# Pooled attention, then a SiLU layer: denominators and numerators of the attention grouped otherwise within a tile

## The chip, the cores and the metric

One Trainium2 chip, one core. The metric is the device time of one execution in microseconds. Engines: PE (TensorE) does the matrix products, ACT (ScalarE) the exponentials, logarithms, SiLU and some copies, DVE (VectorE) sums and products of tiles, POOL (GpSimd) some sums and most loads, SP the stores. Products land in PSUM, which has eight banks; everything else lies in SBUF.

## The reference

Keys and values are averaged over eight neighbouring rows, a softmax attention of 576 queries over 72 pooled keys follows, for 8 batches of 8 heads of width 64. The result, 4608 tokens of 512, goes through two matrix products with a SiLU between them (512 to 2048 to 512).

```python
k_p = k.reshape(B, H, Sp, pool, D).mean(axis=3)
v_p = v.reshape(B, H, Sp, pool, D).mean(axis=3)
scores = scale * np.matmul(q, k_p.transpose(0, 1, 3, 2))
scores = scores - np.max(scores, axis=-1, keepdims=True)
attn = np.exp(scores)
attn = attn / (np.sum(attn, axis=-1, keepdims=True) + 1e-09)
out = np.matmul(attn, v_p)
# x: tokens x 512, heads side by side
h = x @ w_in
g = h * (1.0 / (1.0 + np.exp(-h)))
return g @ w_out
```

## The kernel before

The tokens are worked in nine tiles of 512 (t = 0 to 8), each in two halves. `up` multiplies the tile by `w_in` and applies SiLU; `down`, or from tile 1 on `down_quarters`, multiplies by `w_out` and stores. Three quarters of the hidden units in `up` (from tile 1 on) and all of `down_quarters` use seven products in place of eight, with sums of the operands made on DVE: `x_sum` (L444) for the token side, `h_sum` (L605) for the hidden side. The seven products collect in three PSUM banks named P, Q and R, tag "mm". Product 2 goes to P and 5 to Q, r_sb (ACT) and rr_sb (DVE) take them out, 1 goes to R and t_sb (DVE) takes it out, then 4 and 7 go to P and 3 and 6 to Q. The four results go to `o_sb` by L666, L671, L675 and L679, in this order, and SP stores them.

The attention of batch t + 1 is worked in `down_quarters` of tile t, in small matmuls between the large ones. Its 576 queries are cut into three thirds (`visits`) of 192 tokens, two groups of heads side by side, 384 columns. For each third: `scores` (16 matmuls into four banks, then four exponentials on ACT into `es`), `denominators` (four matmuls with a matrix of ones into one bank, then on ACT `lnd`, a logarithm, and `rec`, the exponential of its negative), and `numerators` (16 matmuls into two banks, then two products with `rec` on DVE, which write `xT`, the tokens of later tiles). These use the PSUM tag "at", which has five banks, used in turn; `up` uses the same five for the P and Q of its units. Tile t + 1 covers the last tokens of batch t and the first of batch t + 1, so in tiles 1 to 5 the last third of a batch is not needed in the next tile, and parts of it are left to that tile's `down_quarters`.

The order on every engine is the order in which the program issues its instructions. `spread` sets it: the 112 matmuls of `down_quarters` are steps 0 to 111, each filler has a step, and a filler is issued as soon as the next step comes up; fillers with the same step keep the order in which they were listed. A filler's ACT, DVE and DMA instructions get their place in their engines' queues at the same moment. Each engine waits in its own order for what its next instruction needs.

In tiles 2 to 5, `down_quarters` has four groups of attention matmuls: scores of third 0 (step 1); denominators of the last third of the batch before, denominators of third 0 and scores of third 1 (33); denominators of third 1, numerators of third 0 and of the last third of the batch before (56); numerators of third 1, into one "mm" and one "at" bank, and scores of third 2 (79.5 and 80). Tile 1 has the same without the batch before. Tile 6 has its scores at 1, 33 and 75, denominators and numerators of its last two thirds at 97 and 101, and also works off batch 6's last third at 33 and 56. Tiles 7 and 8 have no attention. The sums `x_sum` for the next tile's `up` stand at step 92, in tile 6 at 98, in tile 7 at 44.

At the start of the attention ACT loads its table for exponential and logarithm (L400), at the end of it the one for SiLU (L403). In the next `up` POOL first waits for the last `x_sum` (L196, "gate"), then pools k (L190, L193), issues a load of the next k, pools v, and issues the other loads.

Of the kernel before, what the change touches and what calls it, by code (L numbers as in the profile page):

```python
# [36 lines left out]
def kernel(  # L37
# [53 lines left out]
    def ps_tile(shape, dtype, tag, name):  # L91
        return psum.tile(shape, dtype, tag=tag, bufs=banks[tag], name=name)
# [259 lines left out]
    def denominators(b, segs, on_dve=False):  # L352
        st = batches[b]
        w = width(segs)
        es = st["es", segs]
        den_ps = ps_tile([128, 512], FP32, "at", "den_ps")
        for s in range(4):
            nc.tensor.matmul(  # L358
                den_ps[32 * s : 32 * (s + 1), :w],
                lhsT=ones, rhs=es[:, s, :], start=True, stop=True,  # L360
            )
        rec = mid.tile([128, VW], FP32, tag="rec", bufs=4, name="rec")[:, :w]
        if on_dve:
            nc.vector.reciprocal(rec, den_ps[:, :w])
        else:
            lnd = mid.tile([128, VW], FP32, tag="lnd", name="lnd")[:, :w]
            nc.scalar.activation(lnd, den_ps[:, :w], func=AF.Ln)  # L367
            nc.scalar.activation(rec, lnd, func=AF.Exp, scale=-1.0)
        st["rec", segs] = rec
# [262 lines left out]
    def down_quarters(t, fillers, last=False):  # L632
        step = spread(fillers, 7 * 2 * KQ)
        ps = {
            n: ps_tile([128, 2, CQ], FP32, "mm", f"o_ps{n}") for n in "RPQ"
        }
        bank = {2: "P", 5: "Q", 1: "R", 4: "P", 3: "Q", 7: "P", 6: "Q"}
        begun = set()

        def product(n, k0, k1, cs=(0, 1)):  # L640
            b = bank[n]
            for kt in range(k0, k1):
                for c in cs:
                    next(step)
                    nc.tensor.matmul(  # L645
                        ps[b][:, c, :], lhsT=left(n, kt, c), rhs=W_OUT[n][:, kt, :],
                        start=b not in begun,
                        stop=kt == k1 - 1, skip_group_check=True,
                    )
                    begun.add(b)  # L650

        add, sub = ALU.add, ALU.subtract
        tt = nc.vector.tensor_tensor
        KA = KQ // 2
        product(2, KA, KQ)
        product(5, KA, KQ)
        product(2, 0, KA)
        nc.scalar.copy(r_sb, ps["P"])
        product(5, 0, KA)
        tt(out=rr_sb, in0=ps["Q"], in1=r_sb, op=add)  # L660
        for cc in ((0,), (1,)) if last else ((0, 1),):
            cs = slice(cc[0], cc[-1] + 1)
            product(1, 0, KQ, cc)
            tt(out=t_sb[:, cs], in0=ps["R"][:, cs], in1=rr_sb[:, cs], op=sub)
            product(4, 0, KQ, cc)
            nc.scalar.copy(o_sb[1][:, cs, LO], ps["P"][:, cs])  # L666
            tail = last and cc == (1,)
            if tail:
                store(t, 3, LO, (nc.gpsimd,))
            product(3, 0, KQ, cc)  # L670
            nc.vector.tensor_copy(out=o_sb[0][:, cs, HI], in_=ps["Q"][:, cs])  # L671
            if tail:
                store(t, 1, HI)
            product(7, 0, KQ, cc)
            tt(out=o_sb[0][:, cs, LO], in0=ps["P"][:, cs], in1=t_sb[:, cs], op=add)  # L675
            for c in cc:
                store(t, c, LO if tail else FULL, (nc.scalar if tail else nc.sync,))
            product(6, 0, KQ, cc)
            tt(out=o_sb[1][:, cs, HI], in0=ps["Q"][:, cs], in1=t_sb[:, cs], op=add)  # L679
            for c in cc:  # L680
                if tail:
                    store(t, 3, HI, both)
                else:
                    store(t, 2 + c, FULL, (nc.gpsimd if last else nc.sync,))
        for _ in step:
            pass
# [105 lines left out]
    for t in range(NT):  # L792
# [43 lines left out]
        if a < B:  # L836
            q_at = [4, 14, 4, 8] if t > 1 else [24, 25, 26, 2] if t else [82, 84, 86, 88]
            if t == 0:
                for j in range(2):
                    f_up.append((44 + 8 * j, lambda j=j: slot_sums("k", j)))  # L840
                    f_up.append((72 + 8 * j, lambda j=j: select_k(1, j)))
                    f_up.append((72 + 8 * j, lambda j=j: copy_k(1, j)))
                    f_down.append((20 + 10 * j, lambda j=j: slot_sums("v", j)))
                    f_down.append((37 + 3 * j, lambda j=j: select_v(1, j, "at")))
                    f_down.append((37 + 3 * j, lambda j=j: copy_v(1, j)))
            elif t == 1:
                for j in range(2):
                    f_up.append((0, lambda j=j: slot_sums("k", j, halves=True)))
                    f_up.append((22, lambda j=j: select_k(2, j)))
                    f_up.append((23, lambda j=j: copy_k(2, j)))  # L850
                    f_down.append((8, lambda j=j: slot_sums("v", j, halves=True)))
                    f_down.append((40, lambda j=j: select_v(2, j, "at")))
                    f_down.append((41, lambda j=j: copy_v(2, j)))
            else:
                f_up.append((1, behind_x_sums))
                f_up.append((1, lambda: pool_k(a)))
                if a + 1 < B:
                    f_up.append((2, lambda: load_one(a + 1, "k")))
                f_up.append((2, lambda: pool_v(a)))
                f_up.append((40, lambda: k_transpose(a)))  # L860
            for n in range(4):
                f_to = f_down if t and n >= (2 if t > 1 else 3) else f_up
                f_to.append((q_at[n], lambda n=n: q_transpose(a, n % 2, n // 2)))
            if t == 0:
                f_down.append((0, lambda: load_half_2("k", 0)))
                f_down.append((0, lambda: load_q(2)))
                f_down.append((0, lambda: load_half_2("k", 1)))
                for half in range(2):
                    f_down.append((31, lambda half=half: load_half_2("v", half)))
                for y in range(2):  # L870
                    for n in U_W:
                        f_down.append((6, lambda y=y, n=n: unit_weight_sum(y, n)))
            elif a + 1 < B:
                if t == 1:
                    f_up.append((0, lambda: load_one(a + 1, "k")))
                f_to, at = (f_up, 4) if t > 1 else (f_down, 11)
                f_up.append((5 if a + 1 == B - 1 else 0, lambda: load_q(a + 1)))
                f_to.append((at, lambda: load_one(a + 1, "v")))
                f_up.append((5, lambda: load_rest(a + 1, "k")))
                f_to.append((at + 2, lambda: load_rest(a + 1, "v")))  # L880
            f_down.append((0, attn_tables))

            if t:
                sc_at, den_at, nu_at = (1, 33, 80), (33, 56, 97), (56, 79.5, 101)
                if t == B - 2:
                    sc_at, nu_at = (1, 33, 75), (56, 97, 101)
            else:
                sc_at, den_at, nu_at = (1, 16, 30), (16, 30, 44), (44, 55, 56)
            later = 0 < t < B - 2
            if 1 < t < B - 1:  # L890
                f_down.append((den_at[0], lambda: denominators(a - 1, visits[2])))
            for n, sg in enumerate(visits):
                if n < 2 or not later:
                    f_down.append((den_at[n], lambda sg=sg: denominators(a, sg)))
                f_down.append((sc_at[n], lambda sg=sg: scores(a, sg)))

            for n, sg in enumerate(visits):
                tags = ("mm", "at") if later and n == 1 else ("at", "at")
                if n < 2 or not later:
                    f_down.append(  # L900
                        (nu_at[n], lambda sg=sg, tags=tags: numerators(a, sg, tags))
                    )
                if n == 0 and 1 < t < B - 1:
                    f_down.append((nu_at[n], lambda: numerators(a - 1, visits[2])))
        if 0 < t < B:
            for n in (4, 1, 3, 7, 6):
                f_down.append((44 if t == B - 1 else 98 if t == B - 2 else 92, lambda n=n: unit_x_sum(t + 1, n)))
        if t == 1:
            def unit_weight_tiles():
                k_w = big.tile([128, 4, 2, 256], BF16, tag="k_raw2", name="w_sum12")  # L910
# [43 lines left out]
```

## Time and profile before

| | us |
|---|---|
| median of 3 runs | 282.37 |
| lowest, highest | 282.14, 282.44 |
| the profiled execution's own time | 282.37 |
| its span | 280.6 |
| tile 2, 81.31 to 110.40 | 29.09 |
| tile 3, 110.40 to 139.49 | 29.09 |
| tile 4, 139.49 to 168.62 | 29.13 |
| tile 5, 168.62 to 197.70 | 29.08 |
| tile 6, 197.70 to 227.60 | 29.90 |
| tile 7, 227.60 to 252.49 | 24.89 |

| engine | busy, us | share of the span |
|---|---|---|
| PE | 273.7 | 98% |
| DVE | 221.1 | 79% |
| ACT | 189.2 | 67% |
| POOL | 98.3 | 35% |

A tile is taken here from the first matmul of its `up` to that of the next. In the lines below, a row of a timeline gives the start in us, the length, the engine, the line of the kernel, the operation with its result and sources, their shapes, and how many equal instructions were merged; in brackets stands how long the engine was idle before it and which instruction ended that. The ends of matmuls are modelled, and they overlap, so that distances of starts say more than lengths. A row of the waits gives who waited for whom, the total in us, how many times, and the longest.

### The profile page before, as it was taken

What the parts mean: (1) busy time and instruction counts of PE and PEld (TensorE: products, weight loads), DVE (VectorE), ACT (ScalarE), POOL (GpSimd) and SP (SyncE); (2) the same over time, 40 slices, a digit from 0 to 9 for tenths busy, and PEclk for the clock granted to TensorE, in tenths of its full rate; (3) what the DMA queues carried; (4) which work ended last, traced back from release to release, by engine and by line L of the source; (5) the groups of instructions that cost most, each with busy time, mean ns of one, the idle gap of its engine ahead of it and who ended that gap; (6) DMA issues with size and microseconds to landing.
All of it is one profiled execution on the core that took longest, in us unless ns stands there. A gap on an engine that the chain in (4) does not pass through costs nothing.

```text
span 280.6 us, 7165 instructions
## 1 busy us (share of the span) xinstructions
PE 273.7 (98%) x2877; PEld 203.7 (73%) x2877; DVE 221.1 (79%) x415; ACT 189.2 (67%) x369; POOL 98.3 (35%) x104
## 2 busy tenths in 40 slices
PE   8999998999999999999999999999999999999995
PEld 4448444577888777867888788677877878788784
DVE  4996858997898967796879696978788588966982
ACT  1788767468567974797579866995699668426810
POOL 8655217232168233931293109940910000000001
PEclk9999999999999999999999999999999999999999
DMA  7999999897459797789467805998320032005004
GB/s 215 277 258 241 208 313 204 220 197 117 115 75 236 186 130 148 184 167 129 78 161 187 126 11 132 204 112 129 87 66 2 2 94 58 0 5 138 11 2 151
DMA packets 31313, 37.71 MB, mean 134 GB/s; under 512 B 10352, under 2 KB 22256, under 8 KB 31280
## 3 DMA queue, kind: packets, MB, share of 16 engines
q0 software_dynamic: 23920, 27.03, 52.6%
q1 hardware_dynamic: 6928, 9.58, 12.1%
q10 hardware_dynamic: 432, 0.66, 0.6%
q8 instruction: 22, 0.36, 0.6%
q14 instruction: 11, 0.09, 0.1%
HBM read 36.70 MB, written 9.44 MB: 164 GB/s over the span
## 4 chain that ended last, share of the span: by engine, by line
PE 78%; DMA 12%; DVE 4%; POOL 2%; ACT 1%; issue 1%; POOLq 0%; DVEq 0%
PE o_psP L645 16%; PE o_psQ L645 15%; PE u_psP L477 11%; PE hp_ps L537 10%; PE u_psQ L477 10%; DMA raw<-in_v_dram 9%; PE o_psR L645 5%; DMA raw<-in_k_dram 3%; PE u_psR L477 3%; PE sc_ps L340 3%; PE nu_ps L384 2%; PE den_ps L358 1%; DVE w_sum L623 1%; DVE xT L393 1%; ACT lnd L367 1%
## 5 line engine op out<-in xcount | busy, mean ns | idle before, releaser
L645 PEld LDWEIGHTS <-h_sum 128*128 128x128 bf16 x640 | 60.7, 98 | 11.4 <-DVE h_sum L605 1.3
L477 PEld LDWEIGHTS <-w_sum 128*128 128x128 bf16 x460 | 45.0, 98 | 8.4 <-issue 0.5
L537 PE MATMUL hp_ps<-xT,w_in_sb 128*128 128x512 bf16 (+3 forms) x268 | 50.5, 332 | 0.1
L605 DVE TENSOR_TENSOR h_sum<-h_T 128x1024 bf16<-128x1024 bf16 (+1 forms) x72 | 49.7, 743 | 1.0 <-ACT h_T L543 1.0
L348 ACT ACTIVATE es<-sc_ps 72x384 bf16<-72x384 f32 (+1 forms) x100 | 39.1, 470 | 13.5 <-PE sc_ps L340 13.2
L543 ACT ACTIVATE h_T<-hp_ps 128x512 bf16<-128x512 f32 (+2 forms) x63 | 31.7, 520 | 10.3 <-PE hp_ps L537 7.2
L537 PEld LDWEIGHTS <-w_in_sb 128*128 128x128 bf16 x268 | 25.6, 98 | 15.3 <-issue 1.1
L485 ACT ACTIVATE h_T<-c_sb 128x512 bf16<-128x512 f32 x46 | 28.8, 628 | 4.5 <-DVE c_sb L509 3.1
L393 DVE TENSOR_TENSOR xT<-nu_ps,rec 128x384 bf16<-128x384 f32 (+1 forms) x50 | 23.9, 532 | 4.6 <-PE nu_ps L384 4.5
L645 PEld LDWEIGHTS <-h_T 128*128 128x128 bf16 x256 | 24.5, 98 | 3.8 <-issue 0.9
L549 POOL DMA_DIRECT2D out_dram<-o_sb x2 | 1.2, 617 | 70.7 <-issue 70.0
L494 ACT COPY r_sb<-u_psP 128x512 f32<-128x512 f32 x23 | 13.5, 585 | 15.1 <-PE u_psP L477 13.8
L190 POOL TENSOR_TENSOR raw<-raw 72x1024 f32<-72x1024 f32 x10 | 23.6, 2357 | 0.1
L500 DVE TENSOR_TENSOR t_sb<-u_psR,rr_sb 128x512 f32<-128x512 f32 x23 | 15.9, 692 | 8.8 <-PE u_psR L477 7.2
L367 ACT ACTIVATE lnd<-den_ps 128x384 f32<-128x384 f32 (+1 forms) x23 | 11.1, 481 | 12.7 <-PE den_ps L358 12.7
L477 PEld LDWEIGHTS <-w_in_sb 128*128 128x128 bf16 x184 | 17.6, 98 | 2.4
L497 DVE TENSOR_TENSOR rr_sb<-u_psQ,r_sb 128x512 f32<-128x512 f32 x23 | 15.7, 682 | 3.2 <-ACT r_sb L494 1.8
L263 DVE TENSOR_TENSOR raw<-raw 128x384 f32<-128x384 f32 (+3 forms) x20 | 12.4, 619 | 6.9 <-DMA raw<-in_k_dram 3.8
L512 DVE TENSOR_TENSOR c_sb<-u_psQ,t_sb 128x512 f32<-128x512 f32 x23 | 15.8, 687 | 2.4 <-PE u_psQ L477 2.3
L509 DVE TENSOR_TENSOR c_sb<-u_psP,t_sb 128x512 f32<-128x512 f32 x23 | 15.8, 687 | 2.3 <-PE u_psP L477 1.0
L645 PE MATMUL o_psP<-w_out_sb,h_sum 128*128 128x256 bf16 x128 | 17.6, 273 | 0.0
L645 PE MATMUL o_psR<-w_sum,h_sum 128*128 128x256 bf16 x128 | 16.7, 273 | 0.0
(83 smaller groups left out, 513.6 us busy)
## 6 DMA issues: line engine op xcount, KB each, us to landing
out_dram<-o_sb SPq DMA_DIRECT2D x128, 64.0 KB, 1.8
raw<-in_k_dram POOLq DMA_DIRECT2D x10, 576.0 KB, 8.2
raw<-in_v_dram POOLq DMA_DIRECT2D x10, 576.0 KB, 7.9
q_bf<-in_q_dram POOLq DMA_DIRECT2D x6, 576.0 KB, 10.3
w_in_sb<-in_moe_w_in_dram POOLq DMA_DIRECT2D x8, 256.0 KB, 8.1
w_out_sb<-in_moe_w_out_dram POOLq DMA_DIRECT2D x4, 512.0 KB, 13.3
raw<-in_v_dram POOLq DMA_DIRECT2D x2, 768.0 KB, 11.0
raw<-in_k_dram POOLq DMA_DIRECT2D x1, 768.0 KB, 9.8
```

What stands on the lines that cost most here:

```text
L190: nc.gpsimd.tensor_add(out=raw[:, :, : 2 * D], in0=raw[:, :, : 2 * D], in1=raw[:, :, 2 * D :])
L348: nc.scalar.activation(es[:, s, :], sc[s], func=AF.Exp, scale=score_scale)
L393: nc.vector.tensor_mul(out=xT[:, 2 * g0 + c : 2 * (g0 + ng - 1) + c + 1 : 2, cols], in0=nu[c][:, :w].rearrange("r (g n) -> r g n", g=ng), ...
L477: nc.tensor.matmul(ps[y, bank][:, u, :], lhsT=w[:, kk, 128 * u : 128 * (u + 1)], rhs=x[:, kk, :], start=first and u == 0 and kk == 0, stop ...
L485: nc.scalar.activation(h_T[:, g : g + 2, j * NQ : (j + 1) * NQ], src, func=AF.Silu)
L500: tt(out=t_sb, in0=ps[y, "R"], in1=rr_sb, op=ALU.subtract)
L509: tt(out=c_sb[0], in0=ps[y, "P"], in1=t_sb, op=ALU.add)
L512: tt(out=c_sb[1], in0=ps[y, "Q"], in1=t_sb, op=ALU.add)
L537: nc.tensor.matmul(hp_ps[:, r0:r1], lhsT=w_in_sb[:, kk, g * 128 : (g + 1) * 128], rhs=xT[:, kk, x0 : x0 + r1 - r0], start=(kk == 0), stop= ...
L543: nc.scalar.activation(h_T[:, g, n0 : n0 + n], hp_ps[:, :n], func=AF.Silu)
L605: nc.vector.tensor_tensor(out=h_sum[n][:, ks, :], in0=quarter(*a, ks), in1=quarter(*b, ks), op=op)
L645: nc.tensor.matmul(ps[b][:, c, :], lhsT=left(n, kt, c), rhs=W_OUT[n][:, kt, :], start=b not in begun, stop=kt == k1 - 1, skip_group_check= ...
```

## The change

The denominators of a batch's last third are issued in its own tile, at step 97, no longer in the next one; its numerators stay in the next tile at step 56. The numerators of third 1 move from step 79.5 to 97, behind those denominators, and use two "at" banks. Scores of third 1 and denominators of third 0 go from step 33 to 31, scores of third 2 from 80 to 75. The sums of x go from step 92 to 98 in tiles 1 to 5. Tile 6 loses the denominators that it did for batch 6 at step 33, and has its scores of third 1 at 31. The names of the three output banks are made in another order. Tile 0, 7 and 8 are as before. After it, tiles 1 to 5 have five groups: scores of third 0; denominators of 0 and scores of 1; denominators of 1 and two numerators; scores of 2; denominators of 2 and numerators of 1.

```diff
     def down_quarters(t, fillers, last=False):
         step = spread(fillers, 7 * 2 * KQ)
         ps = {
-            n: ps_tile([128, 2, CQ], FP32, "mm", f"o_ps{n}") for n in "RPQ"
+            n: ps_tile([128, 2, CQ], FP32, "mm", f"o_ps{n}") for n in "PQR"
         }
...
             if t:
-                sc_at, den_at, nu_at = (1, 33, 80), (33, 56, 97), (56, 79.5, 101)
-                if t == B - 2:
-                    sc_at, nu_at = (1, 33, 75), (56, 97, 101)
+                sc_at, den_at, nu_at = (1, 31, 75), (31, 56, 97), (56, 97, 101)
             else:
                 sc_at, den_at, nu_at = (1, 16, 30), (16, 30, 44), (44, 55, 56)
-            later = 0 < t < B - 2
-            if 1 < t < B - 1:
-                f_down.append((den_at[0], lambda: denominators(a - 1, visits[2])))
             for n, sg in enumerate(visits):
-                if n < 2 or not later:
-                    f_down.append((den_at[n], lambda sg=sg: denominators(a, sg)))
+                f_down.append((den_at[n], lambda sg=sg: denominators(a, sg)))
                 f_down.append((sc_at[n], lambda sg=sg: scores(a, sg)))
 
             for n, sg in enumerate(visits):
-                tags = ("mm", "at") if later and n == 1 else ("at", "at")
-                if n < 2 or not later:
-                    f_down.append(
-                        (nu_at[n], lambda sg=sg, tags=tags: numerators(a, sg, tags))
-                    )
+                if n < 2 or not 0 < t < B - 2:
+                    f_down.append((nu_at[n], lambda sg=sg: numerators(a, sg)))
                 if n == 0 and 1 < t < B - 1:
                     f_down.append((nu_at[n], lambda: numerators(a - 1, visits[2])))
         if 0 < t < B:
             for n in (4, 1, 3, 7, 6):
-                f_down.append((44 if t == B - 1 else 98 if t == B - 2 else 92, lambda n=n: unit_x_sum(t + 1, n)))
+                f_down.append((98 if t < B - 1 else 44, lambda n=n: unit_x_sum(t + 1, n)))
```

## The prediction

> **What bounds the kernel now.** I read the first table of the page, then the waits by total, then the engines' timelines through one whole tile and through tile 6, which already works as the change wants it.
>
> ```profile
> PE 273.7 (98%) x2877; PEld 203.7 (73%) x2877; DVE 221.1 (79%) x415; ACT 189.2 (67%) x369; POOL 98.3 (35%) x104
> ```
>
> ```profile
> PE sc_ps L340 <- ACT lnd L367: 1.1, 5, 0.2
> ```
>
> TensorE is never without work for long (the windows by tile give 28.9 us busy of 29.1 at clock 1.00), so time comes or goes only as matmuls or as holes in its stream. The list of waits has one hole that repeats, five times: scores waiting for ACT's logarithm. Its 1.1 us counts only what lies after the modelled end of the matmul before; the starts show more. TensorE in tile 3 (start us, length us):
>
> ```profile
> 127.22 0.38 PE L645 MATMUL o_psR<-w_sum,h_sum 128*128 128x256 bf16 x2
> 127.53 0.51 PE L358 MATMUL den_ps<-es,ones 72*32 72x384 bf16 x8
> 127.97 0.28 PE L340 MATMUL sc_ps<-qT,kz 32*72 32x192 bf16 x3
> 128.47 0.50 PE L340 MATMUL sc_ps<-qT,kz 32*72 32x192 bf16 x13 [0.22 <-ACT lnd L367]
> 128.90 1.70 PE L645 MATMUL o_psR<-w_sum,h_sum 128*128 128x256 bf16 x14
> ...
> 134.98 0.27 PE L645 MATMUL o_psP<-w_sum,h_sum 128*128 128x256 bf16 x1
> 135.18 0.52 PE L384 MATMUL nu_ps<-es,vp 72*32 72x192 bf16 x16
> 135.62 0.54 PE L340 MATMUL sc_ps<-qT,kz 32*72 32x192 bf16 x16
> 136.09 1.81 PE L645 MATMUL o_psP<-w_sum,h_sum 128*128 128x256 bf16 x15
> ```
>
> Three score matmuls go, the fourth starts 0.50 us after the third group began. It writes the PSUM bank of the old denominator, and ACT's lnd, 0.49 us from 127.93, empties that bank.
>
> The same place without the old denominator, in tile 1, and then the later groups as tile 6 has them:
>
> ```profile
> 69.65 0.38 PE L645 MATMUL o_psR<-w_sum,h_sum 128*128 128x256 bf16 x2
> 69.96 0.35 PE L358 MATMUL den_ps<-es,ones 72*32 72x384 bf16 x4
> 70.24 0.54 PE L340 MATMUL sc_ps<-qT,kz 32*72 32x192 bf16 x16
> 70.71 0.94 PE L645 MATMUL o_psR<-w_sum,h_sum 128*128 128x256 bf16 x7
> ...
> 220.53 1.47 PE L645 MATMUL o_psQ<-w_sum,h_T 128*128 128x256 bf16 x12
> 221.93 0.54 PE L340 MATMUL sc_ps<-qT,kz 32*72 32x192 bf16 x16
> 222.40 0.61 PE L645 MATMUL o_psQ<-w_sum,h_T 128*128 128x256 bf16 x4
> ...
> 224.60 0.38 PE L645 MATMUL o_psQ<-w_sum,h_sum 128*128 128x256 bf16 x2
> 224.91 0.35 PE L358 MATMUL den_ps<-es,ones 72*32 72x384 bf16 x4
> 225.08 0.50 PE L384 MATMUL nu_ps<-es,vp 72*32 72x192 bf16 x16
> 225.52 0.61 PE L645 MATMUL o_psQ<-w_sum,h_sum 128*128 128x256 bf16 x4
> ```
>
> Here no score waits, and the 16 pass in 0.47 us.
>
> **The change, part by part.** I call the thirds of the batch 0, 1, 2; S, D and N are scores, denominators and numerators; Dp and Np those of the batch before. No matmul is added or dropped over the whole run; groups are cut elsewhere. A group's cost is the distance of starts across it, less the output products in that distance at 0.109 us (16 take 1.75 us in the chain of waits).
>
> - [Dp D0 S1], tiles 2 to 5 and 6: 128.90 − 127.22 − 2 × 0.109 = 1.46.
> - [D0 S1], what is left of it: 70.71 − 69.65 − 0.22 = 0.84.
> - [N1 S2], tiles 1 to 5: 136.09 − 134.98 − 0.11 = 1.00. It is split into
> - [S2] alone: 222.40 − 220.53 − 12 × 0.109 = 0.56, and
> - [D2 N1]: 225.52 − 224.60 − 0.22 = 0.70.
>
> [S0] and [D1 N0 Np] stay. So tile 1 pays 0.56 + 0.70 − 1.00 = +0.26. Tiles 2 to 5 pay 0.84 + 0.56 + 0.70 − 1.46 − 1.00 = −0.36 each, −1.44. Tile 6 loses Dp only, 0.84 − 1.46 = −0.62. Sum −1.80 us. The cost of one more group per tile (entry and exit of the small matmuls) is in these numbers. A check from tiles alone: tile 6 lasts 29.90 us against tile 3's 29.09; it is [S2], [D2 N1] and one more N (225.52 to 226.50 less four products: 0.54) in place of [N1 S2]: 0.56 + 0.70 + 0.54 − 1.00 = 0.80. It was 0.81.
>
> **What else moves, at nothing, and its cover.**
>
> - D0 and S1 two steps sooner (0.22 us). D0's exponents end at 126.96, it would start at 127.31. S1's second half needs the second transpose of q, which ends at 127.35; it would be asked for at about 127.8. Bounds: 0, and 0.36 a tile if a wait of the old size came back. I take 0: tile 1's rows have this group without a wait.
> - D1 needs S1's exponents. On ACT only one lnd and one rec (0.49 and 0.52) stand ahead of them, not two. In tile 1, where that is so already, they end at 72.99 and D1 starts at 73.67. Taking off the two selections of v there (0.35 us) and giving two steps more, 0.55 us is left.
> - S2 five steps sooner takes the banks of D1 and of three numerators. Tile 6 has S2 at that step, with the same four releases: no wait. D2 needs S2's exponents: they end at 224.12, D2 starts at 224.91.
> - lnd and rec of D2 now precede the silu table load (1283 ns) on ACT at the end of tiles 1 to 5; behind it stand r_sb of the next tile's first product, then every silu. On tile 6's clock, with the second numerator group gone (0.54 less), the next tile would start at 227.06. The table is in at 227.73 and r_sb ends at 228.3. TensorE needs it for the product that adds to the same bank, 2.18 us into the tile (229.78 − 227.60 in tile 7), at 229.24: 0.9 us of cover.
> - On DVE, L675 now goes ahead of N1's two products, then five x_sums, then L679, then rr_sb. Tile 6's rows put them at 224.85, 225.48, 226.42 to 228.09; L679 would follow to 228.7 and rr_sb to 229.3. N1's rows of xT are asked for at 227.5 (they end at 226.5), the first x_sum at 229.24 (226.8), bank Q by the third late product at 230.11 (229.3): 0.8 us. Tile 7 starts with two products more in that queue and has no hole.
> - POOL waits in its queue for the last x_sum (L196); behind it stand both poolings and the next loads of k and v, and in tile 5 the eight loads of q. x_sum ends 1.0 us before the tile's start now (138.47 against 139.49) and would end 1.0 us after it. kp would be ready 4.9 us into the tile, kT asks at 8.9; vp is asked for after 20 us. POOL idles 7.9 to 12.5 us at that gate from tile 3 on, so 2 us more do not pass on to the loads. SP's stores of o_sb[0] are issued sooner, and nothing waits for them within the tile.
> - Order of names P, Q, R: in the built program P, Q and R get the same three banks either way, and g0 the same as R. Nothing.
>
> One rule speaks against this. In the trace, the exponents at 125.34 follow a table load of 124.05 to 125.33 at once, so a switch costs 1.28 us here. The Trainium skill (ScalarE: Activation LUTs, "What ACT_TABLE_LOAD costs") puts a drain of 1380 ns on top, 2.66 us a switch. By that r_sb would end near 229.7, TensorE would wait 0.4 us at five starts of a tile, and the sum would be an estimated +0.4 us instead of −1.8; the trace shows no such drain, and I go by its row.
>
> The profiled execution took 282.37 us, of which 280.6 is the span. That is also the median of the three runs. 282.37 − 1.80 = **280.6 us**. 0.2% is 0.56 us, about what a measurement can tell from no change.
>
> **Rivals.**
>
> 1. As worked out, give or take 0.4 us: 0.84.
> 2. A smaller wait takes the place of lnd: S1 waits for the second transpose (cover 0.4 us) or D1 for exponents (0.55 us). For it: both covers are short. Against: tile 1 shows both groups without a hole. At half of the 0.46 us hole in five tiles, 1.2 is given back: 281.7. I give 0.06 to this, 281.0 to 281.8.
> 3. Slower: the DVE queue at the end of the tile becomes the bound. L679 and rr_sb come so late that the next tile's product into bank Q waits. Place: first 3.1 us of tiles 2 to 6. Every 0.1 us beyond the cover of 0.8 costs 0.5 us in all; from 1.27 us late on the kernel is over 0.2% slower, and at 1.4 us it gives 5 × 0.6 − 1.8 = +1.2: 283.6. For it: x_sums and both halves of the output are now packed into the last 4 us, and POOL's poolings start beside rr_sb. Against: tile 7's start, with 1 us more of DVE work ahead, has no hole, and rr_sb takes 0.69 us beside POOL and without it. 0.07.
> 4. The wait is not for the bank but would be met anyhow, and the change does nothing: 282.4 ± 0.5. Against: in the built program the fourth score tile of S1 waits for Dp's lnd alone, and after the change for S0's exponents. 0.03.
>
> **How the numbers follow.** The prediction is case 1. The low end, 280.2, is its sum with the extra group free of entry and exit (0.1 us in four tiles). The high end, 281.9, takes in case 2 and the near edge of 4; left out are 3 and most of 4, under 2 in 10. Faster by over 0.2% is 1 and 2 less a remnant, 0.89; within 0.2% 0.04; slower 0.07.
>
> **What would show it.** Right: no scores waiting for lnd in the list of waits; tiles 2 to 5 last 28.7 us each, tile 6 29.3, tile 1 0.26 more than now; the last [D2 N1] shows as denominators of 4 and numerators of 16 close before each tile's end. Wrong: a hole in TensorE's stream within 3 us of a tile's start, released by rr_sb or r_sb (case 3), or before D1 or S1 (case 2). The prediction fails if the small groups cost more when they stand alone beside POOL's and DMA's traffic, which tile 6 does not have at that place.

## The result, and the profile after

The changed kernel takes 280.72 us (280.58 to 280.84, six runs) against 282.33 (six runs), a ratio of 0.994 with an interval of 0.993 to 0.996: 1.6 us faster. Forecast were 280.6 us and 280.2 to 281.9. The span went from 280.6 to 278.9 us.

TensorE in tile 3 of the changed kernel (start us, length us, engine, line, operation, tiles, shapes, how many):

```profile
126.34 1.04 PE L645 MATMUL o_psQ<-w_out_sb,h_sum 128*128 128x256 bf16 x8
127.31 0.35 PE L358 MATMUL den_ps<-es,ones 72*32 72x384 bf16 x4
127.58 0.54 PE L340 MATMUL sc_ps<-qT,kz 32*72 32x192 bf16 x16
128.05 1.92 PE L645 MATMUL o_psR<-w_sum,h_sum 128*128 128x256 bf16 x16
...
132.60 1.47 PE L645 MATMUL o_psQ<-w_sum,h_T 128*128 128x256 bf16 x12
134.00 0.54 PE L340 MATMUL sc_ps<-qT,kz 32*72 32x192 bf16 x16
134.47 0.61 PE L645 MATMUL o_psQ<-w_sum,h_T 128*128 128x256 bf16 x4
...
136.67 0.38 PE L645 MATMUL o_psQ<-w_sum,h_sum 128*128 128x256 bf16 x2
136.98 0.35 PE L358 MATMUL den_ps<-es,ones 72*32 72x384 bf16 x4
137.15 0.50 PE L384 MATMUL nu_ps<-es,vp 72*32 72x192 bf16 x16
137.59 1.70 PE L645 MATMUL o_psQ<-w_sum,h_sum 128*128 128x256 bf16 x14
```

All 16 scores of third 1 now go in one run, 0.47 us from their first start to the next product. Less the output products at 0.109 us, the group [D0 S1] costs 128.05 − 126.34 − 0.87 = 0.84 us, [S2] 134.47 − 132.60 − 1.31 = 0.56 and [D2 N1] 137.59 − 136.67 − 0.22 = 0.70. No row of scores waiting for lnd is left in the list of waits.

The same kernel by tile, 2 to 6 (stretch, its length, then busy time and instructions of PE, weight loads, DVE, ACT and POOL, clock, DMA share, GB/s):

```profile
81.66:110.39 28.73, 28.73 (x326) 22.62 (x324) 23.33 (x42) 21.98 (x43) 12.66 (x10) 1.00 0.88 171
110.39:139.12 28.73, 28.73 (x326) 22.63 (x324) 23.30 (x42) 22.10 (x43) 12.68 (x10) 1.00 0.72 148
139.12:167.90 28.78, 28.78 (x342) 24.19 (x340) 23.31 (x42) 22.12 (x43) 11.92 (x9) 1.00 0.58 119
167.90:196.63 28.73, 28.73 (x326) 22.64 (x324) 23.31 (x42) 22.10 (x43) 17.31 (x17) 1.00 0.99 137
196.63:225.92 29.29, 29.29 (x343) 22.83 (x340) 23.86 (x44) 22.65 (x43) 7.35 (x5) 1.00 0.18 46
```

Tiles 2 to 5 lose 0.36, 0.36, 0.35 and 0.35 us, tile 6 loses 0.61. Tile 2 starts at 81.66 and not 81.31, 0.35 later: of this 0.07 was there before tile 1's `down_quarters` (its first product at 65.66 against 65.59), and 0.28 is its new group. The profile, with its modelled ends, has PE busy in the whole of each stretch.

The end of tile 3 on DVE, which the third rival made the bound:

```profile
136.92 0.69 DVE L675 TENSOR_TENSOR o_sb<-o_psP,t_sb 128x512 f32<-128x512 f32 x1 [1.11 <-PE o_psP L645]
137.55 1.02 DVE L393 TENSOR_TENSOR xT<-nu_ps,rec 128x384 bf16<-128x384 f32 x2
138.49 1.75 DVE L444 TENSOR_TENSOR x_sum<-xT 128x512 bf16<-128x512 bf16 x5
140.16 0.68 DVE L679 TENSOR_TENSOR o_sb<-o_psQ,t_sb 128x512 f32<-128x512 f32 x1
140.76 0.68 DVE L497 TENSOR_TENSOR rr_sb<-u_psQ,r_sb 128x512 f32<-128x512 f32 x1
```

The tile ends at 139.12, so rr_sb ends 2.32 us into the next one, where 2.24 was worked out (229.3 less 227.06), and no hole follows.

### The profile page after: what moved, and what is told of

It is laid out like the page before. It is cut to its first block, busy times and chain, and to the rows that moved or that the text cites. A ratio compares the mean times of both kernels' runs of the same rounds, so it can differ in the third digit from the quotient of the medians.

```text
span 278.9 us, 7160 instructions
## 1 busy us (share of the span) xinstructions
PE 273.2 (98%) x2877; PEld 203.4 (73%) x2877; DVE 220.6 (79%) x415; ACT 189.2 (68%) x369; POOL 98.4 (35%) x104
## 4 chain that ended last, share of the span: by engine, by line
PE 79%; DMA 14%; DVE 4%; issue 1%; ACT 1%; POOL 0%; DVEq 0%; POOLq 0%
PE o_psQ L645 16%; PE o_psP L645 15%; PE u_psP L477 11%; PE hp_ps L537 11%; PE u_psQ L477 10%; DMA w_in_sb<-in_moe_w_in_dram 6%; DMA raw<-in_v_dram 6%; PE o_psR L645 5%; PE u_psR L477 3%; PE sc_ps L340 3%; PE nu_ps L384 2%; DMA q_bf<-in_q_dram 2%; PE den_ps L358 2%; DVE w_sum L623 1%; DVE xT L393 1%
## 5 line engine op out<-in xcount | busy, mean ns | idle before, releaser
L645 PE MATMUL o_psQ<-w_sum,h_sum 128*128 128x256 bf16 x128 | 16.7, 273 | 0.0
```

What stands on the lines that cost most here:

```text
L645: nc.tensor.matmul(ps[b][:, c, :], lhsT=left(n, kt, c), rhs=W_OUT[n][:, kt, :], start=b not in begun, stop=kt == k1 - 1, skip_group_check= ...
```

## The experiments

A cover, here and in the prediction, is the time by which a thing may come later before another engine waits for it. The ratios are to the kernel before, run again beside each experiment (282.48 to 282.52 us).

**Dp alone, in another place.** Is it the bank that Dp holds, or what else the change brings? Two runs on the kernel before, each with Dp moved and nothing else. The first puts it ahead of D1:

```diff
             if 1 < t < B - 1:
-                f_down.append((den_at[0], lambda: denominators(a - 1, visits[2])))
+                f_down.append((den_at[1], lambda: denominators(a - 1, visits[2])))
```

> The kernel before, with one edit: the denominators of the batch before (Dp) go from step 33, ahead of D0 and S1, to step 56, ahead of D1. Four groups a tile remain, N1 and S2 stay at 79.5 and 80, the x sums at 92. Theory A (S1's fourth bank held by Dp's logarithm is the whole loss): the hole goes, [D0 S1] costs 0.84 us and not 1.46, and four denominators are added to the third group at 0.17, in tiles 2 to 6: 5 x 0.45 = 2.3 us less, 280.1. Now the second product of Np takes Dp's bank and may meet lnd there: the group's PE stream reaches it about 0.8 us after Dp's start, lnd ends about 1.0 after it; if that wait comes, 0.15 x 5 is given back, 280.8. Theory B (the gain of the change came from its new groups, steps or banks, not from where Dp stands): 282.3.

280.73 us, ratio 0.995 (0.994 to 0.996): theory A, with the wait that it left open. The third group in tile 3, of the kernel before and then of this run:

```profile
131.69 0.83 PE L384 MATMUL nu_ps<-es,vp 72*32 72x192 bf16 x32
132.46 0.94 PE L645 MATMUL o_psP<-w_sum,h_T 128*128 128x256 bf16 x7
```

```profile
129.43 1.15 PE L645 MATMUL o_psP<-w_sum,h_T 128*128 128x256 bf16 x9
130.51 0.51 PE L358 MATMUL den_ps<-es,ones 72*32 72x384 bf16 x8
130.84 0.95 PE L384 MATMUL nu_ps<-es,vp 72*32 72x192 bf16 x32
131.73 0.94 PE L645 MATMUL o_psP<-w_sum,h_T 128*128 128x256 bf16 x7
```

From the numerators' first start to the next product it is 0.89 us, where it was 0.77 before: 0.12 more. Dp's logarithm ends at 131.40 here, while the numerators run; whether the 0.12 is a wait for it, the last kernel below decides. Tiles 2 to 5 take 28.74 to 28.79 us and tile 6 29.57. With one edit, four groups and the old steps, it has the whole gain of the change.

The second run puts Dp behind S1:

```diff
                 f_down.append((sc_at[n], lambda sg=sg: scores(a, sg)))
+                if n == 1 and 1 < t < B - 1:
+                    f_down.append((sc_at[n], lambda: denominators(a - 1, visits[2])))
```

> The kernel before, with one edit: Dp stands behind S1 in the same group, not ahead of D0. Theory A: S1 passes without a hole, but Dp now takes D0's bank, so that PE waits for D0's logarithm, which ends about 0.98 us after D0's start, when S1 is through at 0.74: a hole of 0.2 to 0.25 in place of 0.46, and one more change between kinds of small matmul. 0.15 us less in tiles 2 to 6, 281.6. Theory B: 282.3.

282.25 us, ratio 0.999 (0.998 to 1.000): little is left, less than expected (281.6). TensorE in tile 3:

```profile
127.76 0.35 PE L358 MATMUL den_ps<-es,ones 72*32 72x384 bf16 x4
128.04 0.54 PE L340 MATMUL sc_ps<-qT,kz 32*72 32x192 bf16 x16
128.78 0.35 PE L358 MATMUL den_ps<-es,ones 72*32 72x384 bf16 x4 [0.20 <-ACT lnd L367]
129.06 1.70 PE L645 MATMUL o_psR<-w_sum,h_sum 128*128 128x256 bf16 x14
```

The time alone fits theory B (282.3) better than A. The rows decide: S1 passes, and now Dp waits for D0's logarithm, 0.74 us from S1's start to Dp's, 0.27 more than S1 takes. Tiles 2 to 6 gained 0.06 to 0.08 and not 0.15; I had not counted the exit from four denominators to the large product, 0.28 us here where the denominators alone were put at 0.17.

**The change with the old denominators put back,** ahead of D0:

```diff
+            if 1 < t < B - 1:
+                f_down.append((den_at[0], lambda: denominators(a - 1, visits[2])))
             for n, sg in enumerate(visits):
-                f_down.append((den_at[n], lambda sg=sg: denominators(a, sg)))
+                if n < 2 or not 0 < t < B - 2:
+                    f_down.append((den_at[n], lambda sg=sg: denominators(a, sg)))
```

> The changed kernel, with one edit undone: the denominators of the last third go back to the next tile, ahead of D0, at step 31; everything else of the change stays (five groups, N1 at 97, S2 at 75, x sums at 98). Theory A: the hole is back. Tiles 2 to 5: first group +0.62, last group without its denominators -0.17, so +0.45 each; tile 1 -0.17; tile 6 +0.62: +2.25 us on 280.7, 283.0, slower than the kernel before, with scores waiting for lnd five times again. Theory B: 280.7, for all that B names is still there.

283.13 us, ratio 1.002 (1.001 to 1.003). The hole is back as it was, in tile 3:

```profile
127.62 0.51 PE L358 MATMUL den_ps<-es,ones 72*32 72x384 bf16 x8
128.06 0.28 PE L340 MATMUL sc_ps<-qT,kz 32*72 32x192 bf16 x3
128.56 0.50 PE L340 MATMUL sc_ps<-qT,kz 32*72 32x192 bf16 x13 [0.22 <-ACT lnd L367]
129.00 1.27 PE L645 MATMUL o_psR<-w_sum,h_sum 128*128 128x256 bf16 x10
```

Tiles 2 to 5 take 29.19 to 29.23 us, 0.45 to 0.47 more than in the changed kernel, tile 6 29.90, 0.61 more, and the list of waits has scores waiting for lnd five times again. Dp's place decides, then.

**The other half of the change alone,** on the kernel before:

```diff
-                sc_at, den_at, nu_at = (1, 33, 80), (33, 56, 97), (56, 79.5, 101)
+                sc_at, den_at, nu_at = (1, 33, 75), (33, 56, 97), (56, 97, 101)
...
-                f_down.append((44 if t == B - 1 else 98 if t == B - 2 else 92, lambda n=n: unit_x_sum(t + 1, n)))
+                f_down.append((44 if t == B - 1 else 98, lambda n=n: unit_x_sum(t + 1, n)))
```

> The kernel before, with the other half of the change alone: N1 goes to step 97, S2 to 75, the x sums to 98 in tiles 1 to 5; Dp stays ahead of D0 at step 33, so that there are five groups. Theory A: the hole stays, and the split costs what its rows say, [S2] 0.56 and [N1] 0.54 in place of [N1 S2] 1.00: +0.10 in each of tiles 1 to 5, 282.8. Theory B: the gain of the change is here, 280.7.

283.1 us, ratio 1.003 (1.002 to 1.004): slower. Tile 3 (columns as in the table of tiles above):

```profile
110.64:139.83 29.19, 28.97 (x326) 22.62 (x324) 23.28 (x42) 22.09 (x42) 12.68 (x10) 1.00 0.71 140
```

It takes 29.19 us and not 29.09, and scores wait for lnd five times as before, so that the split costs the 0.10 that its rows say. 282.8 was 0.5 above a kernel before of 282.3; beside this run that kernel took 282.48, so that 0.12 of the 0.62 between the medians is more than was expected. Tiles 1 to 5 add up to 0.54.

This run and the one with the old denominators put back differ from each other only in the order of the names P, Q, R, in the banks of N1, and in the step of [Dp D0 S1], 33 or 31. Their tiles 2 to 6 agree to 0.01 us (29.20, 29.19, 29.24, 29.19 and 29.90 against 29.19, 29.20, 29.23, 29.20 and 29.90).

**The old steps in the changed kernel.**

```diff
-                sc_at, den_at, nu_at = (1, 31, 75), (31, 56, 97), (56, 97, 101)
+                sc_at, den_at, nu_at = (1, 33, 80), (33, 56, 97), (56, 97, 101)
```

> The changed kernel with the old steps: D0 and S1 at 33 and not 31, S2 at 80 and not 75. The prediction costed these moves at nothing: 280.7. If S2 at 80 leaves D2 at 97 to wait for its exponents (they would end some 0.25 us before D2): up to 0.3 us in six tiles, 282.

280.98 us, ratio 0.994 (0.993 to 0.996). Its tiles 2 to 6 last 28.73, 28.73, 28.77, 28.73 and 29.28 us, the same as without the edit. The steps are worth nothing, as costed.

**How much the end of the tile bears on DVE.** The last x sum is made two and four times more in tiles 1 to 5:

```diff
+        if 0 < t < B - 2:
+            for _ in range(2):
+                f_down.append((98, lambda: unit_x_sum(t + 1, 6)))
```

> The changed kernel with work added to the DVE queue at the end of tiles 1 to 5: the last x sum is made three times in place of once, 2 x 0.335 us, ahead of L679 and rr_sb. In the profile of the changed kernel rr_sb ends 2.3 us after the start of tile 4 (141.44 against 139.12) and the product that needs its bank is issued 3.05 us after it, so that the cover is 0.7 us. The late queue as priced in the prediction's third rival: all of 0.67 is covered, 280.7 to 280.8. If the cover was not there and DVE already sets the start of the tile: 5 x 0.67 more, 284.1.

> As the run before, with four more x sums, 4 x 0.335 = 1.34 us. By the cover of 0.7 us, 0.6 us is paid at each of five starts of a tile: 280.7 + 3.0 = 283.7, with a hole in PE's stream before the third late product, released by rr_sb. If the queue has more room than the rows show: 280.7.

282.54 us, ratio 1.000 (1.000 to 1.001), and 287.04, ratio 1.016 (1.015 to 1.017): both missed. Each sum was to take 0.335 us, but the added ones start 0.46 us apart. Each lasts 0.42 us, in the row of five they overlap, and the added ones do not. They write the part of `x_sum` that the one before has just written, which is the likely reason; no run separates it from others. DVE with two more at the end of tile 2, with four more at the end of tile 3:

```profile
110.07 2.68 DVE L444 TENSOR_TENSOR x_sum<-xT 128x512 bf16<-128x512 bf16 x7
...
113.33 0.68 DVE L497 TENSOR_TENSOR rr_sb<-u_psQ,r_sb 128x512 f32<-128x512 f32 x1
```

```profile
140.78 3.60 DVE L444 TENSOR_TENSOR x_sum<-xT 128x512 bf16<-128x512 bf16 x9
...
144.95 0.68 DVE L497 TENSOR_TENSOR rr_sb<-u_psQ,r_sb 128x512 f32<-128x512 f32 x1
```

So the queue was 0.93 and 1.85 us later (2.68 and 3.60 against 1.75), not 0.67 and 1.34. What PE paid, first with two more, then with four:

```profile
113.32 0.60 PE L477 MATMUL u_psR<-x_sum,w_sum 128*128 128x256 bf16 x4
114.06 0.60 PE L477 MATMUL u_psQ<-x_sum,w_in_sb 128*128 128x256 bf16 x4
```

```profile
144.04 0.60 PE L477 MATMUL u_psR<-x_sum,w_sum 128*128 128x256 bf16 x4
145.69 0.60 PE L477 MATMUL u_psQ<-x_sum,w_in_sb 128*128 128x256 bf16 x4 [1.05 <-DVE rr_sb L497]
```

Four products at 0.109 are 0.44, so the holes are 0.74 − 0.44 = 0.30 and 1.65 − 0.44 = 1.21. Both put the cover at the same size: 0.93 − 0.30 = 0.63 and 1.85 − 1.21 = 0.64 us. Beyond it each 0.1 us costs 0.1 at each of five starts. The rows had said 0.73; 0.06 of what is missing is the time from rr_sb's end to PE's start (145.63 to 145.69 with four more). With two more, the hole at the start of tile 4 was 0.66 and not 0.30; L679 began 0.34 us late there, and the runs do not show why.

**How much it bears on ACT.** Two more table loads between the one for SiLU and r_sb:

```diff
+        if 2 <= t < B - 1:
+            moe_tables()
+            attn_tables()
         if t != 1:
             moe_tables()
```

> The changed kernel with two more table loads on ACT at the start of tiles 2 to 6, between the load for SiLU and r_sb: they change nothing that is computed. By the rows (1283 ns a load, nothing behind it) r_sb ends 1.28 + 2.57 = 3.85 us after the tile's start, and the product that needs it is asked for at 2.18: about 1.75 us of PE at each of five starts, 280.7 + 8.8 = 289.5. By the Trainium skill's drain on top (ScalarE: Activation LUTs, What ACT_TABLE_LOAD costs; 2.66 us a switch, an estimate) the two loads take 5.3 us: 303. If ACT does not bind there at all: 280.7.

289.35 us, ratio 1.024 (1.023 to 1.026). ACT, then PE, at the start of tile 4:

```profile
142.13 1.28 ACT L403 ACT_TABLE_LOAD   x1
143.42 1.28 ACT L400 ACT_TABLE_LOAD   x1
144.71 1.28 ACT L403 ACT_TABLE_LOAD   x1
```

```profile
144.49 0.60 PE L477 MATMUL u_psP<-xT,w_sum 128*128 128x256 bf16 x4
146.64 0.60 PE L477 MATMUL u_psP<-x_sum,w_in_sb 128*128 128x256 bf16 x4 [1.55 <-ACT r_sb L494]
```

The loads follow each other at 1.29 us, and r_sb starts at 146.00, 1.29 after the last. The hole is 2.15 − 0.44 = 1.71, so that of 2.57 us 0.86 was covered: the prediction had said 0.9. The drain of which the Trainium skill tells (ScalarE: Activation LUTs, "What ACT_TABLE_LOAD costs") does not show here, neither between two loads nor after the last.

**A kernel that takes the gain without the new group.** Dp at 56 as in the first run, and Np's second product in the output bank R, which is free by then:

```diff
-                    f_down.append((nu_at[n], lambda: numerators(a - 1, visits[2])))
+                    f_down.append((nu_at[n], lambda: numerators(a - 1, visits[2], ("at", "mm"))))
```

> The kernel before with Dp at step 56, and a second edit: the second product of Np goes to the free output bank R, not to the bank of Dp. In the run with Dp at 56 alone the third group cost 1.32 us (129.43 to 131.73 less nine products) where before it cost 1.04, so that 0.11 lay beyond four denominators at 0.17: the wait for Dp's logarithm. Theory A (every wait for lnd on a bank is paid by PE, and only those): 0.11 us less in tiles 2 to 6, 280.73 - 0.55 = 280.2, below both kernels. Rival (the 0.11 is the cost of one more kind of small matmul in the group): 280.7.

280.28 us (seven runs, 279.92 to 282.88), ratio 0.993 (0.991 to 0.994), and its tiles 2 to 5 took 28.62 to 28.66 us. Those tiles are from the run of 282.88, the longest, which lost 2.8 us ahead of tile 1's `down_quarters` (its first product at 68.37 against 65.59), where nothing was changed. To set the kernel beside the changed kernel, both ran again on one chip:

> The changed kernel once more, on one chip with the next run, to compare the two: ratio 0.994 to before, tiles 2 to 5 at 28.73 us, tile 6 at 29.29.

> The kernel before with Dp at 56 and Np's second product in the output bank R, once more. Its tiles were 28.63 (2 to 5) and 29.44 (6), and tile 1 lacks the 0.26 of the changed kernel: 4 x 0.10 + 0.26 - 0.15 = 0.5 us below the changed kernel, ratio 0.992 to before. Rival (its lower median was chance): the same as the changed kernel.

The changed kernel 280.64 us, ratio 0.994 (0.993 to 0.996); this one 280.17, ratio 0.992 (0.990 to 0.993). The two intervals meet, but the tiles do not leave it to chance: 28.62, 28.62, 28.67 and 28.63 us against 28.74, 28.73, 28.77 and 28.73, tile 2 starts 0.30 sooner, tile 6 takes 0.15 more. The third group in its tile 3:

```profile
129.29 1.15 PE L645 MATMUL o_psP<-w_sum,h_T 128*128 128x256 bf16 x9
130.37 0.51 PE L358 MATMUL den_ps<-es,ones 72*32 72x384 bf16 x8
130.71 0.83 PE L384 MATMUL nu_ps<-es,vp 72*32 72x192 bf16 x32
131.47 0.94 PE L645 MATMUL o_psP<-w_sum,h_T 128*128 128x256 bf16 x7
```

Numerators to next product are 0.76 us, as in the kernel before, with the same matmuls in the same order as with Dp at 56 alone: the 0.12 was the wait for the bank. This is the fastest of the kernels run here.

## Why the prediction was right

- **The hole and its cause.** Right, and shown from both sides: without Dp ahead of S1 it goes (Dp at 56, and the change), with Dp put back it returns with the same 0.50 us (the run with the old denominators).
- **The sum.** 0.84, 0.56 and 0.70 were the costs of the groups to the hundredth. Tiles 2 to 5 were forecast at −0.36 and gave −0.35 to −0.36, tile 6 at −0.62 and −0.61, tile 1 at +0.26 and +0.28, together −1.75 of −1.80. The span lost 1.7 and the median 1.6 us of the forecast 1.8; 0.07 of that is the start before tile 1, where nothing was changed.
- **The covers.** DVE's queue was forecast to leave 0.8 us; it leaves 0.63. Of the difference, 0.08 is a slip in the sum: rr_sb was counted at 0.6 us, the distance to a next start, where its end comes 0.68 after its start. So the third rival decides sooner than put there: slower by over 0.2% from 0.63 + 0.47 = 1.1 us late on, not 1.27. ACT's 0.9 us measured 0.86. kp was forecast 4.9 us into the tile and was ready 5.0 (POOL's L193 ends at 144.15, less 139.12). The steps at nothing were nothing.
- **The rivals.** None came about. Of the second, a smaller wait in the place of lnd, the changed kernel shows none; the runs with Dp elsewhere show what it looks like, 0.27 behind S1 and 0.12 in Np. The fourth fell with the result, and with the first run.
- **The table load.** The row's 1.28 us, and not the skill's 2.66, was the price to take: r_sb was in time, and the run with more loads bears it out at 1.29 us each.
- **The names P, Q, R.** Not tried by themselves. The two kernels that differ only in them, in N1's banks and in the step of [Dp D0 S1] (the other half of the change, and the old denominators put back) have the same tiles to 0.01 us, so that nothing was right for all of these together.

## What to carry to other kernels

With banks used in turn, an early small tile can delay a later large one only by where it stands in the order: look who takes the bank that a slow reader holds, and put the tile where the next taker comes late. If some tile of the kernel already works as the change wants it, its rows can price the change; here they did so to 0.02 us a tile, the costs of entry and exit of a group included. A cover read from a queue's rows was a little too large here, 0.1 us in 0.7, and a delay beyond it was paid in full at every tile. A time near a rival's forecast does not decide for the rival: the run with Dp behind S1 kept its time because a new wait and a dearer exit took the place of the old wait, and only the rows showed it.

## What the runs showed of the hardware

A sum on DVE that writes the same part of a tile as the one before took 0.46 us, against some 0.34 in a row of sums into different parts (0.93 and 1.85 us for two and four more). From the end of a logarithm on ACT to the matmul that writes its bank, and from rr_sb to its product, some 0.05 us pass (lnd ends at 128.42 in the kernel before, the score starts at 128.47; 0.06 for rr_sb in the run with four more sums). Four denominators before a large product take 0.28 us to the next start, before numerators 0.17 (136.98 to 137.15 in the changed kernel).
